# First half of g of three more tiles turned in 32x32 blocks instead of through TensorE

## The chip, the cores and the metric

The kernel runs on one core of one Trainium2 chip. The metric is the device time of one execution in microseconds (us), lower is better; a comparison is made between medians of several runs. The core has five engines, each with its own in-order queue: PE (TensorE, with PEld for its weight loads), DVE (VectorE), ACT (ScalarE), POOL (GpSimd) and SP (SyncE, here only issuing DMAs).

## The reference, cut to what matters

Three stages, one after the other. Attention with a window of 32 local keys on each side and 32 global keys gives 4 batches x 544 rows x 512; a dense MLP turns every row into g = leaky_relu(x w_in), 2048 wide, and multiplies by w_out; a soft mixture of 32 slots takes logits = x phi over all 2176 rows, a softmax over the rows (which gives the slot inputs) and one over the slots (which combines the slot outputs).

```python
h = x @ w_in
g = np.maximum(0.01 * h, h)
x = g @ w_out
logits = x @ phi
d = softmax over rows of logits;  slot_input = d.T @ x
c = softmax over slots of logits; out = c @ slot_out
```

The kernel never forms g @ w_out for all rows. It multiplies w_out by phi once (pmat, 2048 x 32), so that logits = g pmat, and it carries the sum of d.T g, so that w_out is applied to 32 slots only.

## The kernel before, in words

The 2176 rows are cut in 17 tiles of 128 rows (tiles 0 to 3 are batch 0, 4 to 7 batch 1 and so on; tile 16 holds the global rows). For each tile, `b_X` turns the attention output x on PE and splits it in a high and a low part (xh, xl), and `b_H(t, f)` computes one quarter f of g (512 columns) with 12 matmuls (L688) and a leaky ReLU on ACT (L695). For the logits g has to lie with its 2048 columns on the partitions, so each 128x128 piece must be turned. There are two ways:

- `b_L(t, f)`: four PE transposes into a PSUM bank gtp (L725) and one 128x512 copy to SBUF, gT, by ACT or DVE (L727).
- `blocks(t, f, gs)`: DVE transposes the 32x32 blocks of a quarter in place of the whole (L707, SBUF to SBUF, tile gb), and when both quarters of a half are done, 16 copies of 32x8x32 move the blocks to where they belong (L716, tile g8). For f = 0 and 1 all 16 are on POOL.

Before, tiles 10 to 14 (`BLK`) take the second way for all quarters, tiles 4 to 9 (`HALF`) for f = 0 and 1, straight from `b_H`; tiles 0 to 3, 15 and 16 take the first way.

`b_M(t)` then multiplies the turned pieces by pmat (16 matmuls, L739, bank lg). A chain of small steps follows, which this text calls the sum chain of a tile: lg is copied by DVE to lp (L748), PE sums it over four groups (L754), DVE takes the maximum over the rows (nm, L758; from the second tile on it is joined with the last maximum, L762), ACT takes the exponential (st, L763), DVE copies a strip (L764), PE turns st (L799), DVE copies d (L786), and PE adds d.T g (up, L809, 4 matmuls); DVE folds up into uacc (L814, L818).

Attention runs in steps of two heads: kT and qT are turned (L389), kw is spread out by DVE (L404, L405), scores sc (L433), masked maximum (L445, nmx L451), 8 exponentials on ACT (se, L453), turned again (etp, L472; eT, L476), times values (po, L492; xn, L500). The values' windows vw are loaded by DMA from SP, and for step 6 and later POOL copies the global rows into each window (L200). The global queries have their own steps (gl, gg, get, geg, gpo, gxt).

The first four tiles are peculiar: their g is computed in the order of f, all tiles together, while w_in and w_out are still being converted, and pmat is complete only at about 148 us. So the logits of tiles 0 to 2 come after that, merged with the attention steps 4 to 7 of batch 1: first all of tile 2, then tile 0 beside the rest of tile 3's g, then tile 1; tile 3's follow with the tiles of batch 1. `merge` interleaves two lists by their weights, but the order within each engine's queue is then fixed when the program is built, by a scheduler that works with its own estimates. Each queue runs strictly in that order.

The tiles gb and the parts gT share a pool tag of two buffers ("gT"), g8 has two buffers of its own, gtp shares two PSUM banks (tp) with etp, kTp, qTp and others. A buffer is handed on when its last reader is done.

Of the kernel before, what the change touches and what calls it, by code (L numbers as in the profile page):

```python
# [20 lines left out]
def kernel(  # L21
# [43 lines left out]
    def hb(name):  # L65
        return bank("hb", name, 2)
# [100 lines left out]
    def load_v(n):  # L167
        if n >= len(order):
            return
        b, i = order[n]  # L170
        if n in (2, 3):
            t = wp.tile([P, NW + 2, 2, D], F32, tag="w", name="vw")
        else:
            t = sa.tile([P, NW + 2, 2, D], F32, tag="vw", name="vw", bufs=2)
        if n < NP + 2:
            for h in range(2):
                nc.sync.dma_start(
                    out=t[0:32, :, h, :], in_=v_l[b, 2 * i + h].rearrange("(w k) d -> k w d", k=32)
                )
            nc.sync.dma_start(  # L180
                out=t[96:128, 0], in_=v_g[b, 2 * i:2 * i + 2].rearrange("h k d -> k h d")
            )
            for p in range(1, 3):
                nc.sync.dma_start(out=t[32 * p:32 * p + 32, 0:NW], in_=t[0:32, p:p + NW])
            nc.sync.dma_start(
                out=t[96:128, 1:NW], in_=t[96:128, 0:1].to_broadcast([32, NW - 1, 2, D])
            )
        else:
            for p in range(3):
                for h in range(2):  # L190
                    nc.sync.dma_start(
                        out=t[32 * p:32 * p + 32, 0:NW, h, :],
                        in_=v_l[b, 2 * i + h, 32 * p:32 * p + 32 * NW, :].rearrange(
                            "(w k) d -> k w d", k=32
                        ),
                    )
            nc.sync.dma_start(
                out=t[96:128, 0], in_=v_g[b, 2 * i:2 * i + 2].rearrange("h k d -> k h d")
            )
            nc.gpsimd.tensor_copy(t[96:128, 1:NW], t[96:128, 0:1].to_broadcast([32, NW - 1, 2, D]))  # L200
        vwin[b, i] = t
# [441 lines left out]
    gt = {}  # L643
    ms = {}
    seq = [(b, T) for b in range(B) for T in range(NT)] + [None]
    BLK = range(10, NTT - 2)
    HALF = range(4, 10)
    MOVE = "P" * 16, "PPPPPPDDDDDAAAAA"
    gp = []

# [22 lines left out]
    def b_H(t, f, half=None):  # L673
        xh, xl = xt[t]
        if half != 1:
            if f == 0:
                gt[t] = (
                    xa.tile([P, FF], F32, tag="xn", name="gx", bufs=1) if t in (3, NTT - 1)
                    else sa.tile([P, FF], F32, tag="vw", name="g2", bufs=2) if t == 2
                    else sb.tile([P, FF], F32, tag="g", name="g", bufs=2)  # L680
                )
            hps[0] = hb("hp")
        hp = hps[0]
        w = wi[f]
        lo, hi = {None: (0, KD), 0: (0, KD // 2), 1: (KD // 2, KD)}[half]
        for k in range(lo, hi):
            for n, (a, c) in enumerate(((xh, 0), (xh, 1), (xl, 0))):
                nc.tensor.matmul(  # L688
                    hp, a[:, k, :], w[c][:, k, :],
                    start=(k == 0 and n == 0), stop=(k == KD - 1 and n == 2),  # L690
                )
        if half == 0:
            return
        gs = gt[t][:, 512 * f:512 * f + 512]
        nc.scalar.activation(out=gs, in_=hp, func=AF.Prelu, alpha=0.01)  # L695
        if t in BLK or t in HALF and f < 2:
            blocks(t, f, gs)

    gbl = {}
# [1 line left out]
    def blocks(t, f, gs):  # L701

        if f % 2 == 0:
            gbl[0] = sb.tile([P, 2, 512], F32, tag="gT", name="gb", bufs=2)
            gbl[1] = gp[0].tile([P, 2, 4, P], F32, tag="g8", name="g8", bufs=2)
        gb, g8 = gbl[0], gbl[1]
        nc.vector.transpose(out=gb[:, f % 2], in_=gs)  # L707
        lst[t, f] = g8[:, f % 2]
        if f % 2 == 0:
            return  # L710
        src = gb.rearrange("p f (q c j) -> p (f q) c j", c=4, j=32)
        dst = g8.rearrange("p f q (a j) -> p (f q) a j", j=32)
        for n in range(16):
            a, c = n // 4, (n + n // 4) % 4
            copy = {"P": nc.gpsimd.tensor_copy, "A": nc.scalar.copy, "D": nc.vector.tensor_copy}[MOVE[f // 2][n]]
            copy(dst[32 * c:32 * c + 32, :, a], src[32 * a:32 * a + 32, :, c])  # L716
# [15 lines left out]
    def b_M(t, fs=range(NQ)):  # L732
        if 0 in fs:
            ms["M"] = bank("sm", "lg", 1)
        lg = ms["M"]
        for f in fs:
            gT = lst.pop((t, f))
            for c in range(4):
                ms["b"] = nc.tensor.matmul(  # L739
                    lg[32 * c:32 * c + 32, 0:P], pmat[:, c, f, :], gT[:, c, :],  # L740
                    start=(f == 0), stop=(f == NQ - 1), skip_group_check=True,
                ).ins
        return lg

    def b_D1(t):
        lg = b_M(t, range(2, NQ) if t in BLK else range(NQ))
        lp = sb.tile([P, 2 * P], F32, tag="lp", name="lp", bufs=1)[:, 0:P]
        nc.vector.tensor_copy(lp, lg[:, 0:P])  # L748
        ms["lg"] = lg, lp
# [28 lines left out]
    def b_D2(t):  # L778
        lg, lp = ms["lg"]
        ms["st"] = d_cols(lg[:, P:2 * P], lp)  # L780
        ms["b"] = ms["mm"]
# [85 lines left out]
    def l_items(t):  # L867
        return ([(0.0, lambda: None), (0.6, lambda: b_M(t, range(2)))] if t in BLK else [
            (0.0, lambda: None) if t in HALF else (0.9, lambda: (b_L(t, 0), b_L(t, 1))),
            (0.9, lambda: (b_L(t, 2), b_L(t, 3))),  # L870
        ]) + [
            (1.3, lambda: b_D1(t)),
            (0.3, lambda: b_D2(t)),
            (0.1, lambda: b_D3(t)),
            (1.0, lambda: b_U(t)),
        ]
# [33 lines left out]
    def merge(a, c):  # L910
        ta, tb = sum(x[0] for x in a) or 1.0, sum(x[0] for x in c) or 1.0
        pa = pb = 0.0
        a, c = list(a), list(c)
        while a or c:
            if a and (not c or pa / ta <= pb / tb):
                w, f = a.pop(0)[:2]
                pa += w
            else:
                w, f = c.pop(0)[:2]
                pb += w  # L920
            f()
# [6 lines left out]
    t = wp.tile([P, 4, NT, 2, D], F32, tag="w", name="qk")  # L928
# [51 lines left out]
    s4, s5, s6, s7 = (step(n) for n in range(NP, 2 * NP))  # L980
    h3 = [(2.6, lambda f=f: b_H(3, f)) for f in range(NQ)]
# [4 lines left out]
    xb.append(bctx.enter_context(tc.tile_pool(name="xb", bufs=1, side="right")))  # L986
    gctx = ExitStack()
    gp.append(gctx.enter_context(tc.tile_pool(name="gp", bufs=1, side="right")))
    for x in l_items(2):
        x[1]()  # L990
    load_v(NP + 1)
    l0, l1 = l_items(0), l_items(1)
    merge(l0 + h3[2:] + l1, s4[-1:] + s5 + s6 + s7)
    b_X(NT)
    attn = [None] + [sum((step(n) for n in range(NP * b, NP * b + NP)), []) for b in range(2, B)]
    LB = NTT - 2
# [340 lines left out]
```

## Time and profile before

| what | us |
|---|---|
| median of 3 runs | 515.98 |
| lowest and highest of them | 514.8, 516.91 |
| the profiled execution, its own time | 517.65 |
| span of that execution in the profile | 515.7 |

The span goes from the first instruction to the last; the profiled execution's own time is 1.95 above it. In the profile a group of equal instructions that follow each other is one row, with the start, the time from the first start to the last end, the engine, the line, what is written from what, and the number of them. Behind it stands the idle time of the engine before it, with what ended it. An fp32 matmul counts as two there, a transpose as one.

### The profile page before, as it was taken

The numbers are of one execution on the slowest core, as the hardware profiler recorded it, in microseconds if no ns is written. First come the engines' busy times: TensorE is split into PE (matmuls) and PEld (weight loads), VectorE is DVE, ScalarE is ACT, GpSimd is POOL, SyncE is SP. The second block draws the span as 40 slices with busy tenths as digits, with TensorE's granted clock in tenths as the row PEclk, the third lists the DMA queues.
The fourth block names the chain that finished last, engine by engine and source line by source line (L and its number), as shares of the span: only waits on it lengthen the run. The fifth ranks groups of instructions, "written<-read, shape, count | busy, mean of one in ns | idle before, by whom it ended". The sixth has DMA issues, their size and how long they took to land.

```text
span 515.7 us, 13708 instructions
## 1 busy us (share of the span) xinstructions
PE 469.5 (91%) x5327; PEld 324.7 (63%) x5327; DVE 282.1 (55%) x956; ACT 240.5 (47%) x742; POOL 166.2 (32%) x309
## 2 busy tenths in 40 slices
PE   8867798868998979999999979999999999999993
PEld 5645575546775756666767657778677777633353
DVE  4585868659658476565453646534755531312422
ACT  4676888758845345444154254324433442300222
POOL 2044787453301113406233251406666620000000
PEclk9987899997999999999999999999999999999997
DMA  9989679598867471532431203209820059999977
GB/s 173 198 203 242 194 211 335 171 316 251 185 156 151 128 147 25 104 75 76 104 70 35 56 1 57 85 19 394 324 81 2 1 197 344 377 384 378 304 236 209
DMA packets 122397, 90.26 MB, mean 175 GB/s; under 512 B 75804, under 2 KB 101212, under 8 KB 122332
## 3 DMA queue, kind: packets, MB, share of 16 engines
q1 hardware_dynamic: 119660, 88.33, 60.4%
q10 hardware_dynamic: 2672, 1.05, 0.8%
q8 instruction: 42, 0.69, 0.6%
q14 instruction: 23, 0.19, 0.1%
HBM read 76.68 MB, written 8.65 MB: 165 GB/s over the span
## 4 chain that ended last, share of the span: by engine, by line
PE 65%; DMA 14%; DVE 8%; ACT 7%; issue 2%; SPq 2%; POOL 1%; ACTq 0%; DVEq 0%; POOLq 0%
PE hp L688 32%; PE ehp L1177 3%; PE up L809 3%; DMA rraw<-in_moe_w_in_dram 3%; PE po L492 3%; PE sc L433 3%; PE lg L739 2%; DMA vw<-vw 2%; PE gtp L725 2%; DMA rraw<-in_moe_w_out_dram 2%; ACT se L453 2%; DMA vw<-in_v_l_dram 2%; PE etp L472 2%; PE sop L1253 1%; DMA qk<-in_q_l_dram 1%
## 5 line engine op out<-in xcount | busy, mean ns | idle before, releaser
L688 PE MATMUL hp<-wi,xxh 128*128 128x512 f32 x512 | 167.0, 407 | 4.0 <-ACT g L695 2.6
L688 PEld LDWEIGHTS hp<-wi,xxh 128*128 128x128 f32 x512 | 91.9, 190 | 34.8 <-issue 10.6
L716 POOL COPY g<-gb 32x256 f32<-32x256 f32 x206 | 82.5, 400 | 79.3 <-DVE gb L707 66.6
L688 PE MATMUL hp<-wi,xxl 128*128 128x512 f32 x256 | 100.8, 395 | 0.0
L695 ACT ACTIVATE g<-hp 128x512 f32<-128x512 f32 x60 | 35.2, 592 | 66.3 <-PE hp L688 64.4
L453 ACT ACTIVATE se<-se,nmx 128x128 f32<-128x128 f32 x128 | 49.6, 391 | 21.6 <-DVE nmx L451 18.8
L688 PEld LDWEIGHTS hp<-wi,xxl 128*128 128x128 f32 x256 | 48.4, 189 | 11.8 <-issue 0.8
L200 POOL COPY vw<-vw 32x1664 f32<-32x1664 f32 x10 | 15.7, 1574 | 97.7 <-DMA vw<-in_v_g_dram 68.3
L259 POOL TENSOR_TENSOR wn<-wn,rraw 128x256 int32<-128x256 int32 x32 | 26.2, 834 | 37.0 <-DMA rraw<-in_moe_w_in_dram 25.5
L707 DVE STREAM_TRANSPOSE gb<-g 128x512 f32<-128x512 f32 x32 | 22.4, 705 | 23.0 <-ACT g L695 17.7
L445 DVE CUSTOM_DVE_ANT_0 se<-sc,mask 128x128 f32<-128x128 f32 x128 | 28.9, 284 | 7.1 <-PE sc L433 6.9
L433 PE MATMUL sc<-kw,qT 64*32 64x128 f32 x1024 | 29.7, 284 | 0.5 <-DVE kw L404 0.3
L492 PE MATMUL po<-vw,eT 128*32 128x64 f32 x1024 | 23.7, 228 | 6.2 <-DMA vw<-vw 4.7
L259 POOL TENSOR_TENSOR wo<-wo,rraw 128x256 int32<-128x256 int32 x23 | 18.5, 818 | 26.6 <-DMA wo_f<-wo 4.9
L492 PEld LDWEIGHTS po<-vw,eT 128*32 128x32 f32 x1024 | 18.1, 113 | 13.5 <-issue 10.6
L472 PE MATMUL etp<-identr,se 128*128 128x128 f32 x128 | 22.3, 296 | 4.6 <-ACT gT L727 3.3
L249 ACT ACTIVATE rraw<-rraw 128x256 int32<-128x256 uint32 x55 | 23.3, 433 | 5.8 <-DMA rraw<-in_moe_w_in_dram 4.9
L433 PEld LDWEIGHTS sc<-kw,qT 64*32 64x32 f32 x1024 | 19.4, 109 | 8.1 <-issue 4.4
L453 ACT ACTIVATION_READ_ACCUMULATOR se<-se,nmx 128x1 f32 x128 | 24.3, 189 | 0.0
L476 DVE COPY eT<-etp 128x512 f32<-128x512 f32 x28 | 18.8, 686 | 7.0 <-PE etp L472 6.7
L404 DVE COPY kw<-kT 128x672 f32<-128x672 f32 x32 | 19.0, 631 | 5.3 <-ACT kT L393 5.2
L472 PEld LDWEIGHTS etp<-identr,se 128*128 128x128 f32 x128 | 15.3, 148 | 10.3 <-ACT gT L727 4.0
(227 smaller groups left out, 803.3 us busy)
## 6 DMA issues: line engine op xcount, KB each, us to landing
ew<-in_moe_w_dram SPq DMA_DIRECT2D x23, 1024.0 KB, 8.5
rraw<-in_moe_w_in_dram SPq DMA_DIRECT2D x32, 256.0 KB, 3.5
vw<-in_v_l_dram SPq DMA_DIRECT2D x60, 112.0 KB, 3.6
rraw<-in_moe_w_out_dram SPq DMA_DIRECT2D x23, 256.0 KB, 5.3
ew<-in_moe_w_dram SPq DMA_DIRECT2D x9, 512.0 KB, 9.1
ew<-in_moe_w_dram SPq DMA_DIRECT2D x17, 256.0 KB, 5.2
wo_f<-wo SPq DMA_DIRECT2D x16, 256.0 KB, 3.8
vn<-in_v_l_dram SPq DMA_DIRECT2D x4, 1024.0 KB, 6.4
```

What stands on the lines that cost most here:

```text
L249: nc.scalar.activation(out=m, in_=lo, func=AF.Copy, scale=2.0 ** -29)
L259: nc.gpsimd.tensor_tensor(out=di, in0=di, in1=m, op=ALU.add)
L404: nc.vector.tensor_copy(kw[:, :, 0:96], src)
L433: last_a[0] = nc.tensor.matmul(bks[e][32 * u:32 * u + 32, P * T:P * T + P], qt[64 * e:64 * e + 64, 32 * U:32 * U + 32], kw[win(U) // (NW / ...
L445: nc.vector.tensor_tensor_reduce(out=s[:, T, :], in0=bk[:, P * T:P * T + P], in1=mask[:, 0 if T == 0 else 2 if T == NT - 1 else 1, :], sca ...
L453: exp_last[0] = nc.scalar.activation(out=s[:, T, :], in_=s[:, T, :], func=AF.Exp, bias=nmx[:, e, T:T + 1], accum_out=sm[:, T, e:e + 1],).ins
L472: last_a[0] = nc.tensor.transpose(pt[:, P * T:P * T + P], es[e][:, T, :], ident).ins
L492: last_a[0] = nc.tensor.matmul(pov[32 * u:32 * u + 32, T, e, :], ets[e][:, 32 * U:32 * U + 32], vw[:, win(U), e, :], start=True, stop=True ...
L688: nc.tensor.matmul(hp, a[:, k, :], w[c][:, k, :], start=(k == 0 and n == 0), stop=(k == KD - 1 and n == 2),)
L695: nc.scalar.activation(out=gs, in_=hp, func=AF.Prelu, alpha=0.01)
L707: nc.vector.transpose(out=gb[:, f % 2], in_=gs)
L716: copy(dst[32 * c:32 * c + 32, :, a], src[32 * a:32 * a + 32, :, c])
```

## The change

The quarters f = 0 and 1 of tiles 0, 1 and 3 now also take the second way. Tile 2 stays as it was. Since the pool of g8 does not exist yet when g of these tiles is computed, `blocks` is not called from `b_H` for them but by a new function `late(t)`, at three places: tile 0 ahead of the logits of tile 2, tile 1 after them, tile 3 between the logits of tile 0 and the rest of its own g. `HALF` also makes `l_items` leave out the PE transposes of f = 0 and 1.

```diff
     BLK = range(10, NTT - 2)
-    HALF = range(4, 10)
+    LATE = 0, 1, 3
+    HALF = *LATE, *range(4, 10)
...
-        if t in BLK or t in HALF and f < 2:
+        if t in BLK or t in HALF and t not in LATE and f < 2:
             blocks(t, f, gs)
...
+    def late(t):
+        for f in range(2):
+            blocks(t, f, gt[t][:, 512 * f:512 * f + 512])
+
+    late(0)
     for x in l_items(2):
         x[1]()
+    late(1)
     load_v(NP + 1)
     l0, l1 = l_items(0), l_items(1)
-    merge(l0 + h3[2:] + l1, s4[-1:] + s5 + s6 + s7)
+    merge(l0 + [(0.0, lambda: late(3))] + h3[2:] + l1, s4[-1:] + s5 + s6 + s7)
```

In the changed program line numbers are one higher from L648 on and seven higher from L1001 on. In all, PE issues 120 transposes of L725 in place of 144, ACT 23 copies of L727 in place of 26 and DVE 7 in place of 10, DVE 38 block transposes of L707 in place of 32, and POOL 254 moves of L716 in place of 206. The orders of PE, DVE and ACT differ from the end of the conversion of w_out to the end of batch 2's attention.

PE around the sum chain of tile 2, before. The first row is the sum of lp, L799 turns st, L809 is up; g_846 is g of tile 0, eT, kn, qn and vw belong to attention steps.

```order
L754 MATMUL lg_2116<-lp_2133,s44_77 128x128
L725 MATMUL gtp_2284<-identr_66,g_846 128x128 x4
L725 MATMUL gtp_2291<-identr_66,g_846 128x128 x4
L472 MATMUL etp_2316<-identr_66,se_1899 128x128 x4
L472 MATMUL etp_2323<-identr_66,se_1909 128x128 x4
L389 MATMUL kTp_2330<-identr_66,kn_1834 128x128 x4
L492 MATMUL po_2379<-vw_2160,eT_2321 32x64 x4
L799 MATMUL lg_2116<-identr_66,st_2138 128x128
```

The same place in the changed program:

```order
L755 MATMUL lg_2136<-lp_2153,s44_77 128x128
L800 MATMUL lg_2136<-identr_66,st_2158 128x128
L810 MATMUL up_2174<-g2_894,d_2164 32x512 x4
L740 MATMUL lg_2324<-g8_2091,pmat_95 32x128 x8
L740 MATMUL lg_2324<-gT_2212,pmat_95 32x128 x4
L472 MATMUL etp_2343<-identr_66,se_1899 128x128 x4
```

The transposes, the attention's matmuls and the first values that stood between the sum and the turning of st now stand behind up or are gone; g8_2091 is tile 0's moved half.

DVE in the same place of the changed program; gb_2180 is tile 1's block transpose, sm and rs belong to attention, nm is the maximum of tile 2's sum chain.

```order
L749 COPY lp_2153<-lg_2136 128x128
L708 STREAM_TRANSPOSE gb_2180<-g_870 128x512 x2
L458 TENSOR_SCALAR sm_2266<-sm_2266 128x8
L759 TENSOR_REDUCE nm_2156<-lg_2136 128x1
L459 RECIPROCAL rs_2267<-sm_2266 128x8
L765 COPY st_2158<-lg_2136 32x128
```

The two block transposes of tile 1 stand between lp and nm, where before there were a gT copy and the masked maxima of an attention step.

PE around the sum chain of tile 1 in the changed program (get and geg belong to the global queries, po to attention step 6, of which the rest of the 32 matmuls follows):

```order
L560 MATMUL get_2762<-identr_66,gs_2596 128x128 x4
L755 MATMUL lg_2833<-lp_2850,s44_77 128x128
L800 MATMUL lg_2833<-identr_66,st_2881 128x128
L810 MATMUL up_2956<-g_870,d_2891 32x512 x4
L492 MATMUL po_2695<-vw_2446,eT_2686 32x64 x2
```

and ACT there:

```order
L453 ACTIVATE se_2811,sm_2775<-se_2811,nmx_2774 128x128 x4
L453 ACTIVATE se_2821,sm_2775<-se_2821,nmx_2774 128x128 x4
L764 ACTIVATE st_2881,zt_2882<-lg_2833,nm_2879 128x128
```

Before, 32 score matmuls, the transposes gxt and xtp and eight of L725 stood on PE between tile 1's sum and the turning of its st; now nothing does, and on ACT the eight exponentials of an attention step stand ahead of st.

POOL, from the last conversion of w_out on, in the changed program (gb_2455 is tile 3, vw_2255 and vw_2446 are the windows of steps 6 and 7):

```order
L259 TENSOR_TENSOR wo_1996<-wo_1996,rraw_1800 128x256
L717 COPY g8_2091<-gb_2090 32x8x32 x16
L717 COPY g8_2181<-gb_2180 32x8x32 x16
L200 COPY vw_2255<-vw_2255 32x1664
L717 COPY g8_2456<-gb_2455 32x8x32 x9
L200 COPY vw_2446<-vw_2446 32x1664
L717 COPY g8_2456<-gb_2455 32x8x32 x7
```

Before, the four copies of L200 for steps 6 to 9 followed the conversion directly.

## Rows read from the trace of the kernel before

**Rows 1.** The page, busy time of each engine over the span.
```profile
PE 469.5 (91%) x5327; PEld 324.7 (63%) x5327; DVE 282.1 (55%) x956; ACT 240.5 (47%) x742; POOL 166.2 (32%) x309
```
**Rows 2.** The page, share of each engine in the chain that ended last.
```profile
PE 65%; DMA 14%; DVE 8%; ACT 7%; issue 2%; SPq 2%; POOL 1%; ACTq 0%; DVEq 0%; POOLq 0%
```
**Rows 3.** Busy time in two stretches: PE, PEld, DVE, ACT, POOL, granted clock, DMA, GB/s.
```profile
144.00:195.00 51.00, 45.69 (x857) 32.25 (x851) 35.23 (x152) 23.40 (x90) 4.71 (x3) 1.00 0.66 139
...
210.00:300.00 90.00, 87.41 (x1155) 61.46 (x1153) 48.92 (x202) 36.65 (x134) 27.69 (x56) 1.00 0.30 66
```
**Rows 4.** Groups by form: moves, block transposes, PE transposes; busy us, mean ns, idle before.
```profile
L716 POOL COPY g<-gb 32x256 f32<-32x256 f32 x206 | 82.5, 400 | 79.3 <-DVE gb L707 66.6 <-PE lg L739 3.4 <-DVE cs L792 1.2
L707 DVE STREAM_TRANSPOSE gb<-g 128x512 f32<-128x512 f32 x32 | 22.4, 705 | 23.0 <-ACT g L695 17.7 <-ACT xxh L664 5.2
...
L725 PE MATMUL gtp<-identr,g 128*128 128x128 f32 x112 | 17.1, 280 | 0.5 <-ACT kT L393 0.5
```
**Rows 5.** Timeline, 145 to 158 us, DVE and PE: tile 2's sum chain and round it.
```profile
145.47 0.69 DVE L727 COPY gT<-gtp 128x512 f32<-128x512 f32 x1 [0.59 <-PE ptps L353]
...
146.34 0.66 PE L725 MATMUL gtp<-identr,g 128*128 128x128 f32 x4
146.92 0.42 PE L739 MATMUL lg<-gT,pmat 128*32 128x128 f32 x6
...
151.31 0.49 PE L754 MATMUL lg<-lp,s 128*128 128x128 f32 x2
151.64 1.04 PE L725 MATMUL gtp<-identr,g 128*128 128x128 f32 x8
...
155.90 0.33 PE L799 MATMUL lg<-identr,st 128*128 128x128 f32 x1
...
157.07 1.02 PE L809 MATMUL up<-g,d 128*32 128x512 f32 x5
```
**Rows 6.** Timeline, 184 to 196 us, all engines: exponentials, tile 1's sum chain.
```profile
184.43 0.39 ACT L453 ACTIVATE se<-se,nmx 128x128 f32<-128x128 f32 x1
...
188.73 0.28 DVE L748 COPY lp<-lg 128x128 f32<-128x128 f32 x1
...
190.31 0.27 DVE L758 TENSOR_REDUCE nm<-lg 128x1 f32<-128x128 f32 x1
...
190.81 0.37 ACT L763 ACTIVATE st<-lg,nm 128x128 f32<-128x128 f32 x1
...
193.92 0.18 DVE L786 COPY d<-lg 128x32 f32<-128x32 f32 x1
...
194.15 1.06 PE L809 MATMUL up<-g,d 128*32 128x512 f32 x8 [1.77 <-DVE d L786]
...
195.15 0.73 PE L688 MATMUL hp<-wi,xxh 128*128 128x512 f32 x2
```
**Rows 7.** Timeline, 165 to 206 us, POOL and DVE: DVE copies with POOL still and busy.
```profile
165.64 1.57 POOL L200 COPY vw<-vw 32x1664 f32<-32x1664 f32 x1 [24.82 <-DMA vw<-in_v_g_dram]
...
171.58 1.02 DVE L404 COPY kw<-kT 128x672 f32<-128x672 f32 x2 [2.13 <-ACT kT L393]
...
172.51 0.47 DVE L405 COPY kw<-kgT 128x224 f32<-128x224 f32 x2
...
187.22 1.57 POOL L200 COPY vw<-vw 32x1664 f32<-32x1664 f32 x1 [16.46 <-DMA vw<-in_v_g_dram]
187.35 1.48 DVE L458 TENSOR_SCALAR sm<-sm 128x8 f32<-128x8 f32 x1 [0.42 <-ACT se L453]
...
197.59 0.17 DVE L458 TENSOR_SCALAR sm<-sm 128x8 f32<-128x8 f32 x1 [0.33 <-ACT se L453]
...
203.77 7.20 POOL L716 COPY g<-gb 32x256 f32<-32x256 f32 x16 [6.55 <-DVE gb L707]
203.94 1.21 DVE L404 COPY kw<-kT 128x672 f32<-128x672 f32 x2 [0.23 <-ACT kT L393]
...
205.07 0.82 DVE L405 COPY kw<-kgT 128x224 f32<-128x224 f32 x2
```

## The prediction, made before the changed kernel ran

> **What bounds the kernel now.** I read the busy times of the page first: PE is busy 91% of the span, the next engine 55% [rows 1], and of the chain that ended last 65% is PE [rows 2]. So what shortens PE's queue, or a wait in it, can shorten the whole, if the place where it happens is itself bound by PE. The change touches the stretch from about 144 us (end of the conversion of w_out) to 195 us, where the first quarter of tile 4's g starts [rows 6]. There PE is busy 45.69 of 51 us, so 5.31 us are waits; DVE is busy 35.23, ACT 23.40, POOL only 4.71 [rows 3]. From 210 to 300 us PE waits 2.6 of 90 us [rows 3]: nothing is removed there, and nothing is to be won there beyond that. The granted clock is 1.00 in both stretches, and stays so over the longest wait of 1.77 us [rows 3, 6], so I count no clock effect.
>
> Two kinds of wait are to be seen in the stretch. The sum chain of tile 2 takes from 151.31 (the sum) to 157.07 (up), but PE is busy in most of it, because transposes of tile 0 and attention stand in its queue between the sum and the turning of st at 155.90 [rows 5]. The sum chain of tile 1 ends with PE waiting 1.77 us for d [rows 6].
>
> **Removed.** 24 PE transposes. Eight of them take 1.04 us from the first start to the last end [rows 5], one lasts 0.28 by itself [rows 4], so they start (1.04 - 0.28) / 7 = 0.11 apart and 24 are worth 2.64 us where PE is bound. With the change to another kind of instruction behind it, a group of four occupies PE for 146.92 - 146.34 = 0.58 [rows 5]; six groups are then worth 3.5. I take 2.64 and keep 3.5 for the end of the range. The three copies that ACT loses and the three that DVE loses (0.69 each [rows 5]) are beside PE.
>
> **Added on DVE and POOL.** DVE gets six block transposes of 0.705 [rows 4], 4.2 us, less 3 x 0.69 = 2.1: DVE goes from 35.2 to 37.3 of 51 us. It has room on the average; where the transposes stand is another thing (below). POOL gets 48 moves; 16 take 7.20 us [rows 7], so 21.6 us, in a stretch where it is idle for 46. Tile 0: DVE's copy that stands at 145.47 [rows 5] is preceded now by two transposes and a copy of pv (0.28, as lp), so the second transpose ends at about 145.47 + 0.7 + 0.28 + 0.7 = 147.1 and the moves at 154.4. Tile 1's follow to 161.6, nine of tile 3's to 165.6, when the data of the window of step 6 land [rows 7]: that copy stands ahead of the nine now, so it is not late. Tile 0's moved half is read behind up of tile 2, at about 156.6 by the walk below: a margin of 2.2 us. I cost POOL at nothing; its cover is this margin.
>
> **New waits on PE.** I went through PE's new order from 144 to 195 us with the durations of the rows, letting each instruction start when its engine and its releaser are done (a handoff is 0.05: d ends at 194.10, up starts at 194.15 [rows 6]).
> - Ahead of tile 2's sum: the last column of pmat is turned when DVE and ACT have copied it, and no transposes stand in between any more, 0.5 us. The first remaining group of tile 0 waits for the bank that DVE empties after the masked maxima of the second head, 1.1 us.
> - Tile 2's sum chain. With nothing between sum, st and up, its latency lies bare. lp 0.28 [rows 6]; then the two block transposes of tile 1 on DVE, 1.4, which outlast the sum (0.49 [rows 5]); a small attention operation, 0.17 [rows 7]; nm 0.27, st 0.37 and the reading of its accumulator, about 0.2, the strip 0.28 as lp, the turning 0.33 [rows 5], d 0.18 [rows 6], six handoffs 0.3: 3.8 us, of which PE works some 0.9. New wait 2.9.
> - Behind it: tile 0's second evicted quarter stands behind uacc on DVE, 0.4; the second eT stands behind the block transposes of tile 3, 1.05.
> - Tile 1's sum chain. lp stands behind eight masked maxima, 1.2 us of waiting; then the chain runs bare, and on ACT eight exponentials stand ahead of st, 8 x 0.39 = 3.1 us [rows 6], where before they were long done when the sum came. 3.85 until st is turned, 0.45 until up: 5.5.
> - The first values of the global queries wait for a copy behind uacc, 0.6; gxt waits for xg behind kw, 0.7.
>
> Together 12.75 us of free PE queue. Busy time in the profile counts a matmul's tail, so each of the twelve waits shows about 0.16 less (0.28 - 0.11, rounded): 10.8. **The sum**: -2.64 - 5.31 (the old waits, all counted as gone, since the walk lists every wait anew) + 10.8 = +2.9 us. The same walk read as a time gives less: the first matmul of tile 4's g starts at 195.75 against 195.15 [rows 6], with 0.45 us of later work already done (three matmuls of tile 3's logits, two transposes): +0.15. The two differ because short gaps at a change of instruction stand in one count and not in the other. I take the middle, **+1.5 us**. Made against the profiled span, 515.7 becomes 517.2; that execution was 517.65, above the median. Against the median of 515.98 the forecast is **517.5**. From 195 us on I assume no change; the order differs there too, by waits on both sides, so I allow 1 us either way.
>
> So what PE is relieved of is given back as waits in two chains that the removed transposes used to fill. About 0.5%, 2.6 us, is what a measurement of this kernel can tell from no change; the forecast lies within it.
>
> **A rule weighed, transposes.** The moves and block transposes of a half cost 2 x 0.705 + 7.2 us on two engines against 2 x 0.44 on PE and two copies; what decides is that POOL's time is free here [rows 3]. The Trainium skill, DVE Perf Modes, section on rules for kernel authors, speaks against the change: a 128x128 transpose belongs on TensorE if a PSUM destination will do, and VectorE's is for 32x32 blocks. By that rule alone the forecast would be a loss wherever the moves are waited for; the trace so far has them covered by 2.2 us.
>
> **The rivals.**
> 1. *Faster: PE's relief stays.* If the engines hand over sooner than I walked, so that the two bare chains are no longer than the waits of before, PE wins the 24 transposes: -2.6, or -3.5 with the gaps, 512.5 us. For it: PE is the bound [rows 1, 2], and the exponentials might start earlier, since the score matmuls stand earlier in the new order and ACT is busy for under half of the stretch [rows 3]. Against it: PE's queue is strictly in order and nothing stands between sum and up in either chain.
> 2. *Slower: POOL's moves hold up DVE.* While a POOL copy ran from 187.22 to 188.79, a small DVE operation took 1.48 us, against 0.17 at 197.59 with POOL still; two kw copies beside POOL's moves took 1.21 and 0.82 in place of 1.02 and 0.47 [rows 7]. The new moves fill 147 to 165.6 us and some more, just where DVE sits in the chains. Some twelve small operations (nmx, sm, rs, cs, cnat) each held for up to one move, 0.40 [rows 4], are at most 4.8, half of it on the chain 2.4, and one set of kw copies 0.2 + 0.35: about +3 on top of +1.5, 520.5 us. It decides once the small operations in 147 to 165 us take over 0.3 instead of 0.17. The lower end of this term is 0, since the block transposes and the copies out of PSUM showed no lengthening. A late POOL would add to it: past the 2.2 us of margin PE waits for the moved half. The Trainium skill, SBUF — State Buffer, section on who interferes with whom, calls the port pair that VectorE shares with GpSimd an exclusive lock, held for a whole instruction; the rows of the held operation agree, and by it the price would be that of this rival.
> 3. That the change does not do what it says is excluded by the counts in the new order: 120 transposes for 144.
>
> **How the numbers follow.** The forecast case, PE's relief given back, within 2.6 us of before: 0.46. Rival 1, faster by more: 0.22; the walk has some twenty links, and each may be off by 0.1 to 0.2, the two long chains by a us. Rival 2, or the +2.9 of the longer sum with anything on top: 0.32. The range goes from rival 1's 512.5 to 520.8, rival 2's 520.5 with a part of the allowance behind 195 us.
>
> **What would show it.** In the profile after: PE's row of L725 falls by 24; PE waiting about 2.5 us for st or d at tile 2's up and 4 to 5 us at tile 1's, with exponentials on ACT ahead of st there. The matmuls on tile 0's g8 wait for nothing. The first matmul of tile 4's g starts between 195 and 198 us. Wrong it would be if those two waits are short (then the time falls towards 512.5), if PE waits for POOL's moves, or if DVE's small operations between 147 and 165 us are lengthened.

## The result, and the profile after

The change took 521.63 us (median of 4 runs, 519.5 to 523.7) against 515.39 for the kernel before beside it (513.71 to 516.91): ratio 1.0122, 95% interval 1.0091 to 1.0154. Timed once more beside the experiments, the ratio was 1.0171 (1.0115 to 1.0226). It is slower by 6 to 9 us; 517.5 was predicted, and the range ended at 520.8. The ratios here and below leave out runs more than 1.5% above the fastest of their kernel, and compare with the kernel before timed beside each run, so they can differ from the quotient of two medians. The profiled execution took 521.53 us, its span is 519.4.

The page of the change, busy time by engine and the chain that ended last (they answer to [rows 1, 2]):
```profile
PE 474.1 (91%) x5303; PEld 325.7 (63%) x5303; DVE 283.0 (54%) x959; ACT 239.5 (46%) x739; POOL 185.5 (36%) x357
...
PE 68%; DVE 8%; ACT 8%; DMA 6%; issue 3%; SPq 3%; POOL 2%; ACTq 0%; POOLq 0%; DVEq 0%
```
PE issues fewer instructions than in [rows 1] and is busy for 4.6 us longer: so instructions take longer, or overlap less. The stretches of [rows 3] in the change, columns as there (length, then PE, PEld, DVE, ACT, POOL, granted clock, DMA, GB/s):
```profile
144.00:195.00 51.00, 42.18 (x726) 28.72 (x726) 32.62 (x129) 19.92 (x76) 20.34 (x45) 0.90 0.47 106
210.00:300.00 90.00, 86.86 (x1075) 61.20 (x1067) 48.20 (x202) 34.22 (x123) 27.33 (x53) 0.98 0.30 65
```
The granted clock, 1.00 in both before, is 0.90 and 0.98 now. These windows are fixed in time, but the change reached their start 6 us earlier, so they don't hold the same work. I therefore cut both traces at the same instructions: S, the start of the first gtp behind 130 us (tile 2, ahead of everything that the change moves on PE), that of the up of tile 3 and that of the up of tile 7. Busy time in these two stretches, columns as in [rows 3], first the kernel before, then the change:
```profile
140.77:221.02 80.25, 74.13 (x1257) 53.01 (x1253) 50.56 (x205) 37.31 (x138) 14.49 (x22) 1.00 0.56 118
221.02:322.81 101.79, 98.00 (x1232) 68.72 (x1231) 54.53 (x217) 41.06 (x148) 33.47 (x69) 1.00 0.26 58
```
```profile
134.41:219.87 85.46, 75.39 (x1233) 52.43 (x1229) 51.25 (x208) 36.39 (x135) 33.62 (x69) 0.94 0.50 110
219.87:326.20 106.33, 101.50 (x1232) 71.47 (x1231) 54.74 (x217) 41.12 (x148) 33.94 (x69) 0.97 0.26 55
```
From S to the up of tile 3 the change takes 5.2 us more: PE idles 10.1 us instead of 6.1, and is busy 1.3 us longer with 24 transposes less. From there to the up of tile 7 it takes 4.5 us more, although PE has as many instructions there as before (1232). From the up of tile 7 to the end every profile of this study has 192.6 to 193.7 us. What differs by 6 us in the other direction is the part ahead of S, the loads and the conversion of the weights: it lasted 133.9 to 141.1 us in fifteen profiles, in the kernel before (140.8, then 137.6) as in changed ones, so I don't count it for or against the change.

The timeline of the change, PE, DVE, ACT and POOL, at the places the prediction spoke of (start and duration in us, engine, line; in brackets the wait and what ended it):
```profile
141.05 13.98 POOL L717 COPY g<-gb 32x256 f32<-32x256 f32 x32 [7.03 <-DVE gb L708]
...
146.37 1.29 DVE L708 STREAM_TRANSPOSE gb<-g 128x512 f32<-128x512 f32 x2
...
146.51 0.48 PE L755 MATMUL lg<-lp,s 128*128 128x128 f32 x2
...
147.59 0.13 DVE L458 TENSOR_SCALAR sm<-sm 128x8 f32<-128x8 f32 x1
...
148.77 0.33 PE L800 MATMUL lg<-identr,st 128*128 128x128 f32 x1 [1.78 <-DVE st L765]
...
149.38 1.09 PE L810 MATMUL up<-g,d 128*32 128x512 f32 x8 [0.28 <-DVE d L787]
...
150.26 1.06 PE L740 MATMUL lg<-g,pmat 128*32 128x128 f32 x16
...
178.78 0.40 ACT L453 ACTIVATE se<-se,nmx 128x128 f32<-128x128 f32 x1 [3.29 <-DVE nmx L451]
...
178.96 0.39 PE L755 MATMUL lg<-lp,s 128*128 128x128 f32 x2
...
179.38 0.29 DVE L759 TENSOR_REDUCE nm<-lg 128x1 f32<-128x128 f32 x1 [0.63 <-PE lg L755]
...
181.49 0.39 ACT L453 ACTIVATE se<-se,nmx 128x128 f32<-128x128 f32 x1
...
181.87 0.35 ACT L764 ACTIVATE st<-lg,nm 128x128 f32<-128x128 f32 x1
...
182.78 0.48 PE L800 MATMUL lg<-identr,st 128*128 128x128 f32 x1 [3.44 <-DVE st L765]
...
183.54 1.94 PE L810 MATMUL up<-g,d 128*32 128x512 f32 x8 [0.28 <-DVE d L787]
...
185.25 1.93 PE L492 MATMUL po<-vw,eT 128*32 128x64 f32 x60
...
283.41 1.11 PE L659 MATMUL xtp<-identr,xn 128*128 128x128 f32 x4 [2.27 <-ACT gT L728]
284.45 1.08 PE L740 MATMUL lg<-gT,pmat 128*32 128x128 f32 x16
...
303.92 1.11 PE L472 MATMUL etp<-identr,se 128*128 128x128 f32 x4 [2.56 <-ACT gT L728]
```
Tile 2's chain lies bare for 1.78 + 0.28 us, and tile 1's two block transposes stand in it: the sum is done at 146.99, they are at 147.66. The moved half of tile 0 (g in lg, 150.26) waits for nothing. Tile 1's chain lies bare for 3.44 + 0.28 us: nm is read from the sum at 179.38, but st starts at 181.87, when the last of the eight exponentials that began at 178.78 is through. Then comes what no term of mine had: up takes 1.94 us in place of 1.06 [rows 6], and po x60 1.93 (1.08 in a run below at 2.4 GHz). That is TensorE at the lower of its two levels, 1.2 GHz ("half clock" from here on), right behind the wait. Behind tile 2's wait it is there too, as the granted clock shows (columns as above):
```profile
150.30:153.70 3.40, 3.40 (x42) 2.30 (x35) 2.41 (x6) 0.08 (x1) 3.11 (x8) 0.50 0.41 92
183.50:187.80 4.30, 3.68 (x69) 2.13 (x69) 2.18 (x7) 0.38 (x2) 0.00 (x0) 0.50 0.02 4
```
The same pair, a wait for something that stands behind exponentials on ACT and then instructions of nearly twice their length, is there at 283 and 304 us.

In the kernel before, the second of those places exists too, and its timeline, ACT and PE, shows how the wait is made:
```profile
297.83 0.40 ACT L453 ACTIVATE se<-se,nmx 128x128 f32<-128x128 f32 x1 [3.19 <-DVE nmx L451]
...
301.40 1.05 ACT L727 COPY gT<-gtp 128x512 f32<-128x512 f32 x2
...
302.02 0.66 PE L472 MATMUL etp<-identr,se 128*128 128x128 f32 x4 [3.02 <-ACT gT L727]
```
Eight exponentials (3.1 us) and an eviction stand ahead of two copies out of PSUM, and etp needs the PSUM bank that they empty. Here the clock stayed at 1.00: etp takes 0.66.

### The profile page after: what moved, and what is told of

Same layout as the page of the kernel before. It is cut to its first block, busy times and chain, and to the rows that moved or that the text cites. A ratio compares the mean times of both kernels' runs of the same rounds, so it can differ in the third digit from the quotient of the medians.

```text
span 519.4 us, 13726 instructions
## 1 busy us (share of the span) xinstructions
PE 474.1 (91%) x5303; PEld 325.7 (63%) x5303; DVE 283.0 (54%) x959; ACT 239.5 (46%) x739; POOL 185.5 (36%) x357
## 3 DMA queue, kind: packets, MB, share of 16 engines
q10 hardware_dynamic: 2672, 1.05, 0.8%
## 4 chain that ended last, share of the span: by engine, by line
PE 68%; DVE 8%; ACT 8%; DMA 6%; issue 3%; SPq 3%; POOL 2%; ACTq 0%; POOLq 0%; DVEq 0%
PE hp L689 31%; DMA rraw<-in_moe_w_in_dram 4%; PE up L810 3%; PE sc L433 3%; PE ehp L1184 3%; PE lg L740 3%; PE po L492 3%; PE etp L472 3%; PE gtp L726 3%; ACT se L453 2%; DMA rraw<-in_moe_w_out_dram 2%; DVE se L445 2%; POOL wn L259 1%; PE sop L1260 1%; PE sop L1238 1%
## 5 line engine op out<-in xcount | busy, mean ns | idle before, releaser
L717 POOL COPY g<-gb 32x256 f32<-32x256 f32 x254 | 102.4, 403 | 101.2 <-DVE gb L708 68.4
L708 DVE STREAM_TRANSPOSE gb<-g 128x512 f32<-128x512 f32 x36 | 25.1, 704 | 27.3 <-ACT g L696 21.6
L200 POOL COPY vw<-vw 32x1664 f32<-32x1664 f32 x10 | 15.8, 1578 | 66.2 <-DMA kn<-in_k_l_dram 24.6
L472 PE MATMUL etp<-identr,se 128*128 128x128 f32 x128 | 24.6, 317 | 3.6 <-ACT gT L728 2.6
L472 PEld LDWEIGHTS etp<-identr,se 128*128 128x128 f32 x128 | 17.1, 160 | 10.3 <-ACT gT L728 2.8
```

The costliest lines, as they stand in the source:

```text
L472: last_a[0] = nc.tensor.transpose(pt[:, P * T:P * T + P], es[e][:, T, :], ident).ins
```

## The experiments

Stages of every profile in us, cut as above (tile 3's up, tile 5's, 6's, 7's, all rows of up on PE), and over the timed runs the mean granted clock and the ratio to the kernel before. "Filled" means that useful work was put into the bare chains, "idle work" that work was which nobody reads, "DVE" that copies of tiles 6 and 7 were given to VectorE:

| run | to S | S to up 3 | to up 5 | to up 6 | to up 7 | clock | ratio (95%) |
|---|---|---|---|---|---|---|---|
| before | 140.8 | 80.3 | 49.0 | 20.0 | 32.8 | 0.967 | 1 |
| before, again | 137.6 | 79.8 | 49.0 | 20.0 | 35.7 | | |
| change | 134.4 | 85.5 | 47.1 | 25.3 | 33.9 | 0.961 | 1.0122 |
| change, again | 133.9 | 85.8 | 47.1 | 24.3 | 34.0 | 0.964 | 1.0171 |
| tiles 0, 1 only | 136.5 | 85.2 | 49.1 | 20.0 | 34.5 | 0.968 | 1.0032 (0.9997-1.0067) |
| tile 3 only | 136.2 | 90.2 | 46.9 | 22.7 | 34.4 | 0.955 | 1.0206 (1.0158-1.0254) |
| 24 idle transposes | 137.8 | 85.0 | 49.0 | 20.0 | 35.5 | 0.964 | 1.0092 (1.0057-1.0128) |
| chains filled | 136.5 | 82.7 | 47.1 | 25.2 | 33.9 | 0.956 | 1.0124 (1.0066-1.0183) |
| tiles 0, 1, filled | 134.2 | 80.3 | 49.0 | 20.0 | 35.3 | 0.969 | 1.0014 (0.9982-1.0046) |
| before, filled | 137.8 | 83.9 | 49.3 | 20.0 | 34.6 | 0.963 | 1.0046 (1.0012-1.0079) |
| idle work, tiles 6, 7 | 136.1 | 86.5 | 47.1 | 24.0 | 33.1 | 0.965 | 1.0109 (1.0054-1.0163) |
| idle work, chains | 138.0 | 78.6 | 51.5 | 22.8 | 34.9 | 0.971 | 1.0024 (0.9991-1.0058) |
| change, copies on DVE | 141.1 | 85.5 | 47.1 | 22.7 | 35.7 | 0.956 | 1.0136 (1.0073-1.0198) |
| before, copies on DVE | 134.9 | 81.5 | 49.0 | 20.1 | 30.1 | 0.971 | 0.9911 (0.9875-0.9948) |
| tiles 0, 1, filled, DVE | 137.0 | 78.4 | 49.0 | 20.1 | 29.9 | 0.971 | 0.9914 (0.9874-0.9953) |

**Which tiles cost it.** Two edits of the tuple, (0, 1) in one run and (3,) in the other, with the calls of late() that go with it:
```diff
-    LATE = 0, 1, 3
+    LATE = 0, 1
...
```


> Edit: tile 3 goes back to its transposes on TensorE; tiles 0 and 1 stay with the block transposes. With that the order of the work from tile 4 on is that of the kernel before again (one row differs), while the order of 144 to 195 us is nearly that of the change. Theory A (the loss of the change has two parts of about half each: bare sum chains of tiles 2 and 1 with a half clock behind them, and an order of tiles 8 and 9 that the scheduler chose anew, with a wait and a half clock at 283 and 304 us): about half of the 6.2 us, 518.5, and no half clock between 275 and 310 us. Rival B (all of it is the two bare chains, the rest differs from run to run): 521. Rival C (GpSimd's moves and VectorE's block transposes cost it, by number): two thirds of it, 519.5, with small VectorE operations lengthened in 147 to 165 us.

> Edit: only tile 3 is turned in blocks; tiles 0 and 1 keep their transposes on TensorE, which stand between sum and st of tile 2 as before. The order from tile 4 on is near that of the change. Theory A: the later part alone, about half of the 6.2 us, 518.5, with a half clock between 275 and 310 us. Rival B: 515, no loss, since tile 2's chain is filled. Rival C: one third, 517.5.

Tiles 0 and 1 alone took 516.5 us, tile 3 alone 524.78. So neither rival, and theory A only in that there are two places; its halves are wrong, and the two runs' losses don't add up to the change's. (Its "tiles 8 and 9" at 283 and 304 us are tiles 6 and 7.) With tiles 0 and 1 the first stage keeps nearly all of its loss (85.2), the later ones are near the kernel before's; against theory A there was half clock between 275 and 310 us (0.50 from 303.0 to 306.4). The profiled run was the longest of its twelve (520.25 us), so it may show more of a loss than the others had; the median's 0.3% is less than the stage's 5 us. Tile 3 alone is at least as bad as all three together, and its timeline, DVE and PE, shows the same figure as tile 1's chain, with DVE in ACT's place:
```profile
179.59 0.17 DVE L458 TENSOR_SCALAR sm<-sm 128x8 f32<-128x8 f32 x1 [3.21 <-ACT se L453]
179.67 0.68 DVE L476 COPY eT<-etp 128x512 f32<-128x512 f32 x1
...
180.41 1.11 PE L726 MATMUL gtp<-identr,g 128*128 128x128 f32 x4 [5.03 <-DVE eT L476]
```
sm needs the last exponential, DVE takes its instructions in order, and the copy behind sm, which empties PE's bank, waits along. The scheduler lays the rest of the program anew for each edit: with tile 3 in the tuple PE's rows from tile 4 on are near those of the change (47 and 23 to 25 us to the ups of tiles 5 and 6), without it near those of the kernel before (49 and 20).

**Is PE's relief worth its time?** The change, with transposes that nobody reads where the removed ones stood:
```diff
...
-            (0.0, lambda: None) if t in HALF else (0.9, lambda: (b_L(t, 0), b_L(t, 1))),
+            (0.9, lambda: idle(t)) if t in LATE else (0.0, lambda: None) if t in HALF else (0.9, lambda: (b_L(t, 0), b_L(t, 1))),
```


> Edit: the change with 24 transposes on TensorE added, which stand where l_items had those of tiles 0, 1 and 3, and whose result nobody reads. Block transposes and moves stay as they are. If TensorE's relief were worth its time, this would cost 2.6 us more than the change: 524.2. Theory A: the transposes fill a part of the waits, the order behind is that of the kernel before again (two rows differ), so it is not slower than the change, and by the later part 3 us faster: 518.5, less what the filled chain of tile 1 gives back: 516 to 518.5. Rival C: as the change, 521.6.

519.45 us: with 24 transposes more it is not slower than the change (1.0092 against 1.0122, intervals that overlap), where a paid relief would have made it 524.2; it is slower than theory A had it. The first stage is as long as without them (85.0), so they stand in what would be waits, and the later stages are those of the kernel before's second profile, half clock in tile 7's included.

**Filling the bare chains with work.**
```diff
-    for x in l_items(2):
-        x[1]()
+    l2 = l_items(2)
+    run(*l2[:4], behind(h3[2]), *l2[4:])
...
-    merge(l0 + [(0.0, lambda: late(3))] + h3[2:] + l1, s4[-1:] + s5 + s6 + s7)
+    merge(l0 + [(0.0, lambda: late(3))] + l1[:4] + [behind(h3[3])] + l1[4:], s4[-1:] + s5 + s6 + s7)
```


> Edit: the change, with a quarter of tile 3's first layer (12 matmuls of 0.23 us) put between sum and st of tile 2, and another between sum and st of tile 1. The order from tile 4 on stays that of the change, row by row. Theory A: the chains' 5.2 us of waiting and the half clock behind tile 1's go, so the stretch from 140 us to tile 4 shortens by 5 to 7 us against the change, and only the later part of the loss stays: 516, perhaps 515. Rival B: all of the loss goes and TensorE's relief shows: 513. Rival C: 521, since block transposes and moves are the same.

> Edit: blocks for tiles 0 and 1 alone, and a quarter of tile 3's first layer between sum and st of tile 2 and of tile 1 (as in the experiment that filled the chains of the whole change). The order from tile 4 on is that of the kernel before but for one row. Theory D: no bare chain, so no half clock from them, and 16 transposes less: against the kernel before 1.8 us for these and 1 to 2 us for waits, so 513 to 514.5, with a mean clock of at least 0.967. Rival F (work taken off TensorE is worth nothing here, since the loads set the pace at this place): 516.

> Edit: the kernel before with its 24 transposes, and only the quarters of tile 3's first layer moved into the sum chains of tiles 2 and 1. Theory G: the one wait of 1.8 us at tile 1's up goes, 514 to 515; against the run with blocks for tiles 0 and 1 and filled chains (514.7) it stands within 1 us, since the 16 transposes (1.8 us) that it still has were not seen there as a gain. Rival F' (the transposes are paid in full once the chains are filled): 1.8 us above that run, 516.5.

The first stage went from 85.6 to 82.7 with all three tiles and from 85.2 to 80.3 with tiles 0 and 1; both gains are smaller than 5 to 7. (Two profiles with the same order and the clock at 1.00 all through this stage, "tiles 0, 1, filled" with and without DVE, differ by 1.9 us, so 2.9 is not far above what a single profile can tell.) In the whole time the first gain doesn't show (521.15), the second may (514.71 against 516.5, intervals that overlap). But the ratio is 1.0014: with 16 transposes less and filled chains the kernel is no faster than before. Its first stage shows why: PE is busy 1.3 us less there than in the kernel before and idle 1.4 us more. So rival F is as near as theory D, though not for its reason: of the waits over 0.25 us in this stage none ends on a load. Busy time in the first stage, columns as in [rows 3], tiles 0 and 1 filled, and then the kernel before filled:
```profile
134.17:214.47 80.30, 72.83 (x1240) 50.40 (x1236) 51.74 (x207) 36.48 (x136) 27.04 (x53) 1.00 0.58 118
```
```profile
137.77:221.62 83.85, 76.34 (x1256) 52.98 (x1252) 51.83 (x208) 37.12 (x138) 14.48 (x22) 0.96 0.55 113
```
The kernel before doesn't gain by the filling, it loses (518.0): its chains were filled by the transposes, and new waits came elsewhere. Beside it the run without 16 of the transposes is 3.3 us faster by the medians (taken on different chips), 1.7 by the ratios, whose intervals overlap; so rival F' may be nearer than theory G, but that the relief is paid in the whole time is not shown. In the stage PE idles 7.5 us in both, and the 3.5 us between their busy times are in part half clock (0.96). At a clock of 1.00 PE is busy 72.83 us without 16 transposes and 74.13 with them (unfilled): 0.08 each.

**The two kernels once more.**

> The kernel before, unchanged, for a second profile. In 23 timed runs beside the four experiments so far its mean granted clock was 0.967 (the change: 0.961, tile 3 alone: 0.955), while the profiled run of it showed 0.973 and 1.00 all through 130 to 320 us. If the first profile was a lucky one, this one shows one or two stretches of half clock between 130 and 320 us, and the first layer of tile 4 at another time than 195 us, with the same order. If its 1.00 is the rule, it shows none.

> The change, unchanged, timed on the chip of these experiments. Theory D (most of the loss is TensorE at 1.2 GHz in pieces of some 3.4 us behind waits of 1.8 us and more, four of them between 145 and 310 us): ratio 1.012, mean granted clock 0.959 against 0.967 of before. Rival E (the waits themselves are the loss): the same ratio, but the clock's mean differs from before's by less than 0.003.

The second profile of the kernel before has the same stages up to tile 6 within 0.5 us, and then, in PE's timeline:
```profile
298.50 1.12 PE L472 MATMUL etp<-identr,se 128*128 128x128 f32 x4 [3.09 <-ACT gT L727]
```
The same wait, 3.09 us for 3.02, and this time etp takes 1.12: the stage to tile 7 is 35.7 us in place of 32.8. So the profile that I predicted from was a lucky one at this place; a wait of 3 us may or may not be followed by half clock. The Trainium skill, TensorE: Matmul & The Clock Gate, section What's actually happening, has the clock set by a monitor that does not start anew with the kernel, so that the point at which the clock changes varies from run to run. The two rows agree. In the runs that the ratio of 1.0171 compares, the change's mean clock was 0.964 and the kernel before's 0.968: half of what theory D asked, and more than rival E allowed. By an estimate 0.0044 of 519 us, some 2 us, is what that clock can cost; so it is hardly most of the loss: theory D falls in its size, and rival E in its claim that there is no such part (next).

**Half clock apart from waits.** Idle work in the waits leaves their length and keeps PE busy, in one run in b_M (the products with pmat) for tiles 6 and 7, in the other in b_D2 (between sum and st) for tiles 1 and 2, where u_add, which makes up, then takes the bank of the idle work:
```diff
+            if f == 1:
+                for _ in range({6: 18, 7: 20}.get(t, 0)):
+                    nc.tensor.transpose(lg[:, 3 * P:4 * P], ident, ident)
...
+        n = {1: 13, 2: 6}.get(t, 0)
+        if n:
+            ms["up0"] = hb("up")
+            with tc.issue_after(ms["mm"]):
+                for _ in range(n):
+                    warm(ms["up0"])
```


> Edit: the change, with 18 transposes of the identity that nobody reads put into TensorE's queue in each of the waits of tiles 6 and 7 (2.27 us at 283 and 2.56 us at 304 in the change's profile); the order is otherwise the change's but for 13 rows. No useful work moves. Theory D: the two stretches of half clock behind these waits go, each 1.7 us, so 3.4 us less than the change, and the mean clock rises by 0.006. Rival E: no gain, 0 to 0.5 us more than the change, since the waits are as long as before.

> Edit: the change, with matmuls on the identity that nobody reads put into TensorE's two bare waits, into the PSUM bank that up overwrites next: 6 of them between sum and st of tile 2, 13 between sum and st of tile 1. The order from 134 us to the up of tile 3 is otherwise the change's; later it is another. Theory J (in this stretch the waits are 4.0 us longer than before the change and half clock costs another 3 to 4, less some 2 for the transposes): the stretch from the first gtp behind 130 us to the up of tile 3 shortens from 85.5 and 85.8 us to 82 to 83, its granted clock is 1.00 or 0.99, and the chains' own instructions end no sooner than before. Rival K (half clock stands there mostly while TensorE waits and costs nothing): 85 to 86 as in the change.

In tiles 6 and 7 the clock was 1.00 to their ups: the stages took 24.0 and 33.1 us, for 25.3 and 33.9 in the change's first profile and 24.3 and 34.0 in its second. The time was 519.83, 1.8 and 3.1 us below the change's two medians where 3.4 was expected; the ratios' intervals overlap, and the mean clock is 0.965 for 0.964, not 0.006 higher. So theory D's direction shows in the stages, its size does not. (The idle transposes write to the bank in which the logits of tiles 6 and 7 are being summed; this kernel doesn't compute the right ones.) In the chains: busy time from S to the first gpo, where both have the same rows but for the idle ones, first the change, then the change with idle work:
```profile
134.41:188.36 53.95, 44.86 (x749) 30.23 (x745) 33.66 (x135) 21.72 (x84) 22.17 (x50) 0.91 0.44 105
```
```profile
137.99:189.23 51.24, 45.98 (x768) 31.58 (x764) 33.74 (x135) 21.71 (x84) 22.47 (x50) 1.00 0.53 110
```
The clock goes from 0.91 to 1.00 and the stretch is 2.7 us shorter, with 19 matmuls more. The three other profiles with the change's order in this stretch (the change again, idle work in tiles 6 and 7, copies on DVE) take 53.7 to 54.3 us at 0.90 to 0.94. The timeline of PE with idle work at tile 1's chain (the lines of st and up are six higher in this file):
```profile
182.71 2.21 PE L85 MATMUL up<-identr 128*128 128x512 f32 x9
185.38 0.33 PE L806 MATMUL lg<-identr,st 128*128 128x128 f32 x1 [0.45 <-DVE st L765]
185.99 1.06 PE L816 MATMUL up<-g,d 128*32 128x512 f32 x8 [0.28 <-DVE d L793]
186.87 1.08 PE L492 MATMUL po<-vw,eT 128*32 128x64 f32 x60
```
up and po are back at 1.06 and 1.08. Theory J is right in its mechanism and rival K is out: of the first stage's loss some 2.7 us are half clock, by one profile against four. (The 78.6 in the table is less than theory J's 82 to 83 and less than that explains; behind the gpo the scheduler laid this run in yet another order.) The whole took 517.07 us, with other stages changed too.

**Taking the exponentials out of the way.** The transposed quarters of tiles 6 and 7 copied by VectorE, in the change, in the kernel before, and in tiles 0 and 1 filled:
```diff
-        (ev or (nc.vector.tensor_copy if f % 2 and not (t >= 6 and f in (1, 3, 9)) else nc.scalar.copy))(
+        (ev or (nc.vector.tensor_copy if t in (6, 7) or f % 2 and not (t >= 6 and f in (1, 3, 9)) else nc.scalar.copy))(
```


> Edit: the change, and the two transposed quarters of tiles 6 and 7 that ACT copied out of PSUM behind eight exponentials are copied by VectorE, which sat idle there for 3.2 us. The order is the change's but for 9 rows. Theory G (both parts of the loss are one thing: TensorE's queue bare at a place where ACT has eight exponentials ahead of the one operation that TensorE needs, and a half clock behind some of these waits): the waits of 2.3 to 2.7 us at 283 and 304 us shrink to 1.2 or less, no half clock between 275 and 310 us, and the time is 3 to 4.5 us below the change: 517.5. Rival H (VectorE's copies come as late, behind its masked maxima, or push the evictions behind them): 521.5 to 522.5.

> Edit: the same copies on VectorE in the kernel before, blocks as before. There only tile 7's wait stood (3.0 us at 302, with a half clock behind it in the second of its two profiles). Theory G: this wait shrinks to 1.2 or less, 1.8 us and the half clock's 1.7 in those runs that have it: 513 to 514. Rival H: 516.

> Edit: blocks for tiles 0 and 1, the filled chains of tiles 2 and 1, and VectorE's copies for tiles 6 and 7. Theory G: 3 us below the same without the copies (514.7): 511.5, under the kernel before. Rival H: 514.5.

In the kernel before it took 511.49 us, less than the 513 to 514 expected, with tiles 0 and 1 512.34: both faster than the kernel before, and equal to each other (0.9911 and 0.9914), so here too 16 transposes less don't show in the whole time. The stage to tile 7 is 30.1 and 29.9 us, its clock 1.00; from the up of tile 3 to that of tile 7 PE idles 1.1 us in the kernel before with these copies, where it idled 3.8 of 101.8 without:
```profile
216.46:315.67 99.21, 98.10 (x1233) 68.91 (x1232) 56.91 (x221) 39.13 (x144) 33.35 (x69) 1.00 0.27 59
```
In the change the time stayed, 523.42. At tile 6 theory G held (0.55 us idle, stage 22.7 for 24.3 to 25.3), at tile 7 rival H, by the timeline of ACT, DVE and PE:
```profile
304.14 0.40 ACT L453 ACTIVATE se<-se,nmx 128x128 f32<-128x128 f32 x1 [2.98 <-DVE nmx L451]
...
307.36 0.17 DVE L458 TENSOR_SCALAR sm<-sm 128x8 f32<-128x8 f32 x1 [3.19 <-ACT se L453]
...
307.84 0.71 DVE L708 STREAM_TRANSPOSE gb<-g 128x512 f32<-128x512 f32 x1
308.48 1.25 DVE L728 COPY gT<-gtp 128x512 f32<-128x512 f32 x2
...
309.19 1.12 PE L472 MATMUL etp<-identr,se 128*128 128x128 f32 x4 [4.04 <-DVE gT L728]
```
In this order the copies stand behind sm on DVE, so they wait for the same exponentials there, and for a block transpose on top.

## Why the prediction was wrong

- **Removed**: right in number (L726 has 96 + 24 transposes, 120 for 144), too high in price: 24 x 0.11 = 2.64 was expected, 0.08 each was measured, 2 us.
- **POOL at nothing**: right. Tile 0's sixteen moves began at 141.05, at 0.44 each they end at 148.0, and the reader came at 150.26: a margin of 2.2 us, as worked out, and no wait. DVE's block transposes held nm of tile 2 by some 0.6 us, which the walk had in its chain. So the rule weighed got its loss, but not because the moves were waited for.
- **Rival 2**: it was the one that ended nearest in time (520.5), but by luck: its mechanism is there with hardly any size. Of the small operations beside the moves three take about 0.1 longer than without (cnat 0.36 for 0.24). The one that was held (0.82 for zacc at 158.41, 0.22 elsewhere) ran beside the copy of a value window, which the kernel before has too. No wait of PE in this stage ends on any of them. Rival 1 fell with the waits of the next point.
- **New waits on PE**: right in place and cause, and close in size: 2.06 us for 2.5 to 2.9 at tile 2, 3.72 for 4 to 5.5 at tile 1 with the exponentials ahead of st, 0.88 for 1.1, 0.37 for 0.5, 0.58 for 0.6; 0.84 for 1.2 ahead of tile 1's sum, 0.34 for 1.05 and 0.12 for 0.7 came out smaller. From S to the first matmul of tile 4's g, the end of the forecast's stretch, idle time went from 5.31 to 9.21 us, +3.9; 5.5 was forecast (10.8 - 5.31). In that sum 0.28 - 0.11 is 0.17, not 0.16, and the list names ten or eleven waits, not twelve; it moves the 10.8 by at most 0.3.
- **The middle, +1.5**: failed. Of two counts, +2.9 and +0.15, I took the mean. By the measured terms waits and transposes are 4 - 2 = +2; the walk's +0.15 was the wrong one.
- **"I count no clock effect"**: the step that failed most. The first stage lost 2.7 us to half clock. That the clock was 1.00 over a wait of 1.77 us says nothing of one of 3.4, nor of the next one of the same length: tile 2's 1.78 was followed by half clock in the change, and the same wait of 1.77 us in the run with tiles 0 and 1 alone was not (1.00 from 151.5 to 180.9).
- **"From 195 us on I assume no change, ±1"**: failed. The scheduler put tiles 6 and 7 in another order, whose waits lie behind exponentials: to the up of tile 7 it took 106.3 and 105.4 us in place of 101.8 and 104.6, so 1 to 4.5 us, depending on where half clock followed a wait, the one of the kernel before included.
- First matmul of tile 4's g "between 195 and 198 us": it stood at 193.83, and 59.4 us behind S for 54.4 before. An absolute time was a poor test, with 7 us of spread ahead of S.

Together: first stage +2 by waits and transposes, +2.7 by clock, against +5.2 to +6 measured, so 0.5 to 1.3 us of it have no name; behind it +1 to +4.5. Whether the part ahead of S differs at all stays open: two profiles of each kernel, with that spread, can't tell.

## What to carry to other kernels

Cut traces of two versions at the same instructions before comparing them: here fixed windows hid a loss of 5 us behind an earlier start, and stages of the same order at the same clock repeat mostly within 0.6 us (1.9 in the worst pair) while the whole varies by 10 (510.1 to 520.4 in 23 runs of the kernel before). Work that is taken off an engine bound in order is worth its time only if the queue behind it isn't waiting for a chain; look at what the removed work was covering, and at what stands ahead of that chain's operations on the other engines (here eight exponentials of 3.1 us, on ACT directly or on DVE behind sm). Waits of 1.8 to 3.4 us on TensorE were followed by half clock in some profiles here and not in others, and where it followed it cost up to 2.8 us more: price it in. Where a scheduler lays the program, every edit is also a new order far from it: look at the waits there too.

## What the runs showed of the hardware that was not expected

- The same wait, 3.02 and 3.09 us in two runs of one program, was followed by 2.4 GHz in one (etp 0.66 us) and by 1.2 GHz in the other (1.12), which cost 2.8 us to the next tile's up.
- Idle matmuls in two waits made this stretch shorter than leaving the waits empty: 51.24 us from S to the first gpo in place of 53.95.
- The mean granted clock of the whole run moved between 0.955 (tile 3 only, 524.78 us) and 0.971 (copies on DVE, 511.49 us): broadly it falls as the times rise, with exceptions (0.964 at 522.91 us, 0.971 at 517.07).
